# Score products of a chunked retention as 64 by 64 quarters instead of 64 by 128 halves

## The chip, the cores and the metric

The kernel runs on one core of one Trainium2 chip. The metric is the device time of one execution in microseconds (us), the median of several runs.

## What is computed

A retention layer (linear attention with a decay per head) and two MLPs behind it, all in fp32. The layer, with 2 sequences, 8 heads, 768 positions and 64 values per head:

```python
for t in range(S):
    state = gamma[None, :, None, None] * state + np.einsum('bhd,bhe->bhde', k[:, :, t], v[:, :, t])
    y[:, :, t] = scale * np.einsum('bhd,bhde->bhe', q[:, :, t], state)
```

Then x = y as 1536 tokens of 512 values, `h = x @ w_in; x = (h * tanh(softplus(h))) @ w_out`, and a second MLP with `h * cos(h)` in the middle, 2048 hidden values each.

## The kernel before

The retention is done in 12 chunks of 128 positions (6 for each sequence). For a chunk `g` TensorE does four sets of fp32 products, each for 4 pairs `a` of heads and both heads `e` of a pair:

- `att_scores` (line 319): scores transposed, keys by queries. A head has 64 of the 128 partitions of `qk` (its two heads lie one above the other). The stationary operand is k, 64 partitions by 128 keys, the moving operand q, 64 partitions by 128 queries. Each head of the pair writes a PSUM tile of its own, `ss[e]`.
- `att_inter` (line 365): what the carried state gives. Stationary is the state of a head, 64 by 64, moving its scaled q, 64 by 128. `rows(a, e)` puts the even pairs and the odd pairs crosswise, so that four products in a row stand in the four 64 by 64 quarters of the array.
- `att_update` (line 334): k and scaled v, 128 positions by 64 columns, added to the state's sum.
- `att_out` (line 375): v (128 by 64 columns) and the masked scores, 128 moving columns.

VectorE multiplies the scores with the decaying mask (`att_mask`, line 328, two for each chunk), ScalarE and GpSimd scale v (`att_vd`) and q (`att_qd`), ScalarE or VectorE read the state's sum (`att_state`), and both take the output into x (`att_x_high`, `att_x_low`). The chunk loads `qkv` (two halves of 512 KB each, `att_load`, line 281) go out on SyncE's queue in order, among them the first MLP weights.

The order of all work is made by a planner (`Plan`): each operation is entered with an engine, a guessed cost and what it needs; TensorE and, for the loads, SyncE keep the order in which operations are entered. Around the change that order is written out as a loop: scores one chunk ahead, then the chunk's other products.

```python
chunk_pre(0)
chunk_scores(0)
...
for n in range(NCHK):
    if n + 1 < NCHK:
        chunk_pre(n + 1)
        chunk_scores(n + 1)
    chunk_inter(n)
    chunk_update(n)
    chunk_out(n)
```

The first chunk of a sequence (0 and 6) has no `att_inter`, the last one (5 and 11) no `att_update`. Behind the last `att_out` the MLPs follow: `gemm1` (line 428 multiplies x and a slice of `w_in` into `ps_h`) and `gemm2` (line 451, `ps_o`), with fp32r operands in a high and a low part, 512 moving columns. The weights' parts are made on VectorE, ScalarE and GpSimd meanwhile (`w_high_part`, `w_low`, `w_low_part` at line 262).

## Time and profile before

| | |
|---|---|
| Median of 3 runs | 572.5 us (572.11 to 572.55) |
| The profiled execution | 573.28 us |
| Its span on the core | 571.5 us |
| TensorE matmuls (PE) busy | 565.8 us, 99% of the span, 3054 instructions |
| TensorE weight loads (PEld) busy | 468.4 us, 82% |
| VectorE (DVE) busy | 382.6 us, 67% |
| ScalarE (ACT) busy | 230.1 us, 40% |
| GpSimd (POOL) busy | 97.5 us, 17% |

The profile records one execution by the hardware. PE is a matmul, PEld the load of its stationary operand, which runs beside other matmuls; matmuls overlap, so a share of 99% says that there is hardly a gap, not that the array is at its peak. In a row of the trace `64*128` after the operation are the rows and columns of the array that it uses, `64x128 f32` the operand; "idle before" in square brackets is time in which the engine stood still just before, with what ended it. "SPq" is SyncE's queue of transfers.

### The profile page before, as it was taken

The numbers are of one execution on the slowest core, as the hardware profiler recorded it, in microseconds if no ns is written. First come the engines' busy times: TensorE is split into PE (matmuls) and PEld (weight loads), VectorE is DVE, ScalarE is ACT, GpSimd is POOL, SyncE is SP. The second block draws the span as 40 slices with busy tenths as digits, with TensorE's granted clock in tenths as the row PEclk, the third lists the DMA queues.
The fourth block names the chain that finished last, engine by engine and source line by source line (L and its number), as shares of the span: only waits on it lengthen the run. The fifth ranks groups of instructions, "written<-read, shape, count | busy, mean of one in ns | idle before, by whom it ended". The sixth has DMA issues, their size and how long they took to land.

```text
span 571.5 us, 7260 instructions
## 1 busy us (share of the span) xinstructions
PE 565.8 (99%) x3054; PEld 468.4 (82%) x3054; DVE 382.6 (67%) x416; ACT 230.1 (40%) x284; POOL 97.5 (17%) x74
## 2 busy tenths in 40 slices
PE   8999999999999999999999999999999999999997
PEld 6888888888888888888888888888888888888886
DVE  5779889662375427653487985898498894765462
ACT  3574543422303303214326465465345354354240
POOL 6680001111110301111101111032010312010000
PEclk9999999999999999999999999999999999999999
DMA  8982254422032200412021030304004010000113
GB/s 297 413 335 75 75 210 158 147 75 73 1 131 91 73 1 0 148 73 75 0 75 73 26 123 1 138 10 147 1 0 148 32 41 2 1 1 1 73 38 110
DMA packets 14721, 49.91 MB, mean 87 GB/s; under 512 B 1632, under 2 KB 2016, under 8 KB 14688
## 3 DMA queue, kind: packets, MB, share of 16 engines
q1 hardware_dynamic: 14688, 49.44, 23.4%
q8 instruction: 24, 0.39, 0.3%
q14 instruction: 9, 0.07, 0.0%
HBM read 46.29 MB, written 3.15 MB: 86 GB/s over the span
## 4 chain that ended last, share of the span: by engine, by line
PE 94%; DMA 4%; SPq 1%; ACT 0%; issue 0%; DVE 0%; ACTq 0%
PE ps_h L428 46%; PE ps_o L451 46%; DMA qkv<-qkv_dram 4%; SPq L294 1%; PE ps_y L381 1%; PE ps_y L370 1%; PE ps_s L325 1%; PE ps_u L341 0%; ACT vd L308 0%; ACT x L395 0%; DVE acc L517 0%; SPq L758 0%; ACT st L353 0%; ACTq L308 0%
## 5 line engine op out<-in xcount | busy, mean ns | idle before, releaser
L428 PE MATMUL ps_h<-x,wi 128*128 128x512 f32 x1152 | 264.8, 389 | 0.0
L428 PEld LDWEIGHTS ps_h<-x,wi 128*128 128x128 f32 x1152 | 216.1, 188 | 45.0 <-issue 0.2
L451 PE MATMUL ps_o<-wo,g 128*128 128x512 f32 (+1 forms) x588 | 132.5, 385 | 0.0
L451 PE MATMUL ps_o<-g,wo 128*128 128x512 f32 x576 | 132.3, 389 | 0.0
L451 PEld LDWEIGHTS ps_o<-wo,g 128*128 128x128 f32 x588 | 108.9, 188 | 22.1
L451 PEld LDWEIGHTS ps_o<-g,wo 128*128 128x128 f32 x576 | 108.1, 188 | 22.5
L494 DVE TENSOR_TENSOR g<-mish,g 128x1024 fp32r<-128x1024 f32 x24 | 33.4, 1393 | 59.2 <-ACT g L490 59.2
L262 POOL TENSOR_TENSOR wo<-mag,wo 128x1024 fp32r<-128x1024 f32 x14 | 35.8, 2557 | 212.8 <-ACT wo L248 212.8
L510 DVE TENSOR_TENSOR acc<-ps_o,acc 128x1024 f32<-128x1024 f32 x35 | 42.8, 1222 | 34.6 <-PE ps_o L451 34.4
L262 POOL TENSOR_TENSOR wi<-mag,wi 128x1024 fp32r<-128x1024 f32 x12 | 30.3, 2525 | 193.1 <-ACT wi L248 193.1
L461 ACT ACTIVATE mish<-ps_h 128x1024 f32<-128x1024 f32 (+1 forms) x25 | 24.9, 995 | 95.1 <-PE ps_h L428 95.1
L474 DVE SCALAR_TENSOR_TENSOR turns<-whole,turns 128x1024 f32<-128x1024 f32 x24 | 29.4, 1223 | 44.7 <-ACT whole L470 44.7
L466 ACT ACTIVATE turns<-ps_h,quarter 128x1024 f32<-128x1024 f32 x24 | 26.7, 1114 | 65.4 <-PE ps_h L428 65.1
L239 DVE SCALAR_TENSOR_TENSOR mag<-raw,mag 128x1024 uint32<-128x1024 uint32 (+1 forms) x38 | 42.2, 1110 | 1.1
L483 ACT ACTIVATE turns<-turns 128x1024 f32<-128x1024 f32 x24 | 25.5, 1062 | 34.8 <-DVE turns L480 34.6
L494 DVE TENSOR_TENSOR g<-turns,g 128x1024 fp32r<-128x1024 f32 x24 | 33.2, 1384 | 8.0 <-ACT g L490 8.0
L486 DVE TENSOR_TENSOR turns<-turns,ps_h 128x1024 f32<-128x1024 f32 x24 | 29.2, 1216 | 10.1 <-ACT turns L483 6.8
L254 DVE SCALAR_TENSOR_TENSOR mag<-raw,mag 128x1024 uint32<-128x1024 uint32 x26 | 33.7, 1301 | 0.4
L490 ACT CAST g<-turns 128x1024 fp32r<-128x1024 f32 x24 | 25.1, 1044 | 16.9 <-DVE turns L486 16.9
L248 ACT CAST wi<-mag 128x1024 fp32r<-128x1024 f32 (+1 forms) x20 | 17.5, 876 | 27.3 <-DVE mag L254 22.4
L470 ACT ACTIVATE whole<-turns,magic 128x1024 f32<-128x1024 f32 x24 | 27.7, 1153 | 0.8
L480 DVE TENSOR_SCALAR turns<-turns 128x1024 f32<-128x1024 f32 x24 | 27.0, 1126 | 0.8
(50 smaller groups left out, 330.2 us busy)
## 6 DMA issues: line engine op xcount, KB each, us to landing
qkv<-qkv_dram SPq DMA_DIRECT2D x24, 512.0 KB, 10.1
raw<-w1i_dram SPq DMA_DIRECT2D x16, 512.0 KB, 4.2
raw<-w1o_dram SPq DMA_DIRECT2D x16, 512.0 KB, 4.1
raw<-w2i_dram SPq DMA_DIRECT2D x16, 512.0 KB, 4.0
raw<-w2o_dram SPq DMA_DIRECT2D x16, 512.0 KB, 3.6
out_dram<-acc SPq DMA_DIRECT2D x11, 256.0 KB, 2.1
out_dram<-acc SPq DMA_DIRECT2D x2, 128.0 KB, 1.7
few<-consts_dram SPq DMA_DIRECT2D x1, 146.0 KB, 2.2
```

The source lines that it names most:

```text
L239: nc.vector.scalar_tensor_tensor(out=a, in0=high, scalar=0xC0000000, in1=a, op0=ALU.bitwise_and, op1=ALU.bitwise_or)
L254: nc.vector.scalar_tensor_tensor(out=w_all_of(it, single)[:, ns], in0=raw_t[it][:, ns, :, 0], scalar=29, in1=mag_t[it][:, ns], op0=ALU.log ...
L262: eng.tensor_sub(out=w[:, :, 1], in0=w_all_of(it, single)[:, ns].bitcast(F32), in1=w[:, :, 0].bitcast(F32))
L428: nc.tensor.matmul(h[:, 0 if h_tag(k) == "s" else f % 2, :], w[:, f % 2, a, kk * 128 : (kk + 1) * 128], x[:, b, kk, :], start=(a + b + kk ...
L451: nc.tensor.matmul(ps, lhs, rhs, start=(n == 0), stop=(n == 3 * GF - 1))
L466: nc.scalar.activation(out=t_t[k], in_=h_t[k], func=AF.Identity, scale=INV_2PI, bias=quarter)
L470: nc.scalar.activation(out=n_t[k], in_=t_t[k], func=AF.Identity, bias=magic)
L474: nc.vector.scalar_tensor_tensor(out=t, in0=n_t[k], scalar=MAGIC, in1=t, op0=ALU.subtract, op1=ALU.subtract)
L480: nc.vector.tensor_scalar(out=t, in0=t, scalar1=-0.5, scalar2=0.5, op0=ALU.max, op1=ALU.min)
L486: nc.vector.tensor_mul(out=t_t[k], in0=t_t[k], in1=h_t[k])
L494: nc.vector.tensor_sub(out=g[:, :, 1, :], in0=t_t[k], in1=g[:, :, 0, :].bitcast(F32))
L510: nc.vector.tensor_add(out=acc, in0=o_t[m * NG + G, j, p], in1=acc)
```

## The change

Each score product is cut in two along the keys: `t` takes 64 of the 128 keys as stationary columns, and writes the 64 partitions of the PSUM tile that belong to them. The moving operand is the same for both. So a chunk has 16 products of 64 by 64 with 128 moving columns instead of 8 of 64 by 128; in the four products that follow each other each stands in another quarter of the array. Nothing else is changed, and no cost or need that the planner sees.

```diff
         for a in range(NPAIR):
-            for e in range(2):
-                h = slice(D * e, D * e + D)
-                nc.tensor.matmul(ss[e][:, a, :], qk[h, a, 1, :], qk[h, a, 0, :], start=True, stop=True)
+            for t in range(2):
+                keys = slice(D * t, D * t + D)
+                for e in range(2):
+                    h = slice(D * e, D * e + D)
+                    nc.tensor.matmul(
+                        ss[e][keys, a, :], qk[h, a, 1, keys], qk[h, a, 0, :], start=True, stop=True, skip_group_check=True,
+                    )
```

On TensorE before, in the middle of the retention (`ps_s` are scores, `ps_y` an output with the carried state at line 370 and with masked scores at line 381, `ps_u` the state's sum; the sizes are those of the product's output):

```order
L381 MATMUL ps_y<-p,qkv 64x128 x8
L325 MATMUL ps_s<-qkv 128x128 x8
L341 MATMUL ps_u<-vd,qkv 64x64 x8
L381 MATMUL ps_y<-p,qkv 64x128 x8
L325 MATMUL ps_s<-qkv 128x128 x8
L370 MATMUL ps_y<-qd,st 64x128 x8
L341 MATMUL ps_u<-vd,qkv 64x64 x8
```

The same place with the change, whose lines are numbered a little higher:

```order
L385 MATMUL ps_y<-p,qkv 64x128 x8
L327 MATMUL ps_s<-qkv 64x128 x16
L345 MATMUL ps_u<-vd,qkv 64x64 x8
L385 MATMUL ps_y<-p,qkv 64x128 x8
L327 MATMUL ps_s<-qkv 64x128 x16
L374 MATMUL ps_y<-qd,st 64x128 x8
L345 MATMUL ps_u<-vd,qkv 64x64 x8
```

The sets of products stand in the same order; only the scores are 16 with an output of 64 by 128 instead of 8 with 128 by 128. The orders of the other engines are the same as before, instruction by instruction.

## Rows read from the trace of the kernel before

**Rows 1.** Page, slices: busy tenths in 40 slices of the span, granted clock, DMA engines.

```profile
PE   8999999999999999999999999999999999999997
...
PEclk9999999999999999999999999999999999999999
DMA  8982254422032200412021030304004010000113
```

**Rows 2.** Chain that ended last, in order of time: start us, us, what.

```profile
17.44 11.76 DMA qkv<-qkv_dram
...
29.28 0.61 ACT vd L308 x3
...
32.07 0.99 PE ps_y L370 x16
...
45.72 32.89 PE ps_h L428 x144
```

**Rows 3.** Waits of SyncE's queue, 0 to 60 us: total us, times, longest.

```profile
SPq L294 <- DMA qkv<-qkv_dram: 13.8, 13, 2.6
```

**Rows 4.** Timeline of weight loads, 31 to 46 us: start us, us, instructions [idle before].

```profile
34.48 0.97 PEld L325 LDWEIGHTS ps_s<-qkv 64*128 64x128 f32 x16 [0.17 <-issue]
35.58 0.43 PEld L370 LDWEIGHTS ps_y<-qd,st 64*64 64x64 f32 x16
36.17 0.55 PEld L341 LDWEIGHTS ps_u<-vd,qkv 128*64 128x64 f32 x16 [0.17 <-issue]
36.63 0.86 PEld L381 LDWEIGHTS ps_y<-p,qkv 128*64 128x64 f32 x16
37.66 0.97 PEld L325 LDWEIGHTS ps_s<-qkv 64*128 64x128 f32 x16 [0.17 <-issue]
...
40.84 0.97 PEld L325 LDWEIGHTS ps_s<-qkv 64*128 64x128 f32 x16 [0.17 <-issue]
...
44.02 0.43 PEld L370 LDWEIGHTS ps_y<-qd,st 64*64 64x64 f32 x16 [0.17 <-issue]
44.62 0.85 PEld L381 LDWEIGHTS ps_y<-p,qkv 128*64 128x64 f32 x16 [0.17 <-issue]
45.65 0.53 PEld L428 LDWEIGHTS ps_h<-x,wi 128*128 128x128 f32 x3 [0.17 <-issue]
```

**Rows 5.** Weight loads by line, 0 to 46 us: count | busy us, mean ns | idle.

```profile
L325 PEld LDWEIGHTS ps_s<-qkv 64*128 64x128 f32 x192 | 11.7, 187 | 3.8 <-DMA qkv<-qkv_dram 2.2 <-issue 1.4 <-PE ps_y L381 0.3
...
L370 PEld LDWEIGHTS ps_y<-qd,st 64*64 64x64 f32 x160 | 4.5, 132 | 1.7 <-issue 0.6
```

**Rows 6.** Timeline of weight loads, 9 to 32 us.

```profile
15.64 0.97 PEld L325 LDWEIGHTS ps_s<-qkv 64*128 64x128 f32 x16 [0.17 <-issue]
...
18.82 0.97 PEld L325 LDWEIGHTS ps_s<-qkv 64*128 64x128 f32 x16 [0.17 <-issue]
...
28.02 1.00 PEld L325 LDWEIGHTS ps_s<-qkv 64*128 64x128 f32 x16 [0.29 <-PE ps_y L381]
...
30.63 0.97 PEld L325 LDWEIGHTS ps_s<-qkv 64*128 64x128 f32 x16 [0.17 <-issue]
```

**Rows 7.** Timeline of ScalarE, 20 to 70 us.

```profile
35.35 2.04 ACT L308 ACTIVATE vd<-qkv,cst 128x64 f32<-128x64 f32 x8
37.27 0.93 ACT L353 ACTIVATE st<-ps_u,cst 128x64 f32<-128x64 f32 x4
```

**Rows 8.** Timeline of GpSimd, 20 to 70 us.

```profile
41.15 1.59 POOL L316 TENSOR_TENSOR qd<-qkv,cst 64x256 f32<-64x256 f32 x2
```

**Rows 9.** Timeline of VectorE, 20 to 70 us.

```profile
43.27 0.42 DVE L350 TENSOR_TENSOR st<-ps_u,cst 128x256 f32<-128x256 f32 x1 [0.40 <-PE ps_u L341]
43.62 0.68 DVE L332 TENSOR_TENSOR p<-ps_s,cst 128x512 f32<-128x512 f32 x1
...
45.15 0.69 DVE L262 TENSOR_TENSOR wi<-raw,wi 128x512 fp32r<-128x512 f32 x1
```

**Rows 10.** Windows, 46 to 60 us: busy us of PE, PEld, DVE, ACT, POOL, clock, DMA.

```profile
46.00:60.00 14.00, 14.00 (x63) 11.57 (x62) 13.59 (x24) 7.33 (x12) 0.00 (x0) 1.00 0.37 132
```

## The prediction

> **What bounds the kernel now.** I read the slices of the page first. TensorE is busy in nearly every slice and its granted clock is full in all of them, while the DMA engines are full in the first slices only [rows 1]. The changed line runs in the first 46 us, so the question is what bounds that stretch. The chain of waits answers in two parts [rows 2]. Up to 29.2 us the chain is loads of `qkv`; behind them stand 2.9 us on ScalarE (the scaled v of chunk 7, a copy of x, the state of chunk 6), and the first TensorE piece starts at 32.07 us. From there to the end the chain is TensorE without a gap. The loads keep their own pace: SyncE's queue waits on earlier loads 13 times, 13.8 us in all [rows 3]. So before 32.07 us time saved on TensorE is time it will wait; after it, time saved is time off the end.

> Which score products stand behind 32.07 us? In the list of weight loads by time, those of chunks 9, 10 and 11, which start at 34.48, 37.66 and 40.84 us, each followed by an `att_inter` [rows 4]. Those of chunks 0 to 8 stand ahead (chunk 8's at 30.63 us [rows 6]).

> How TensorE spends a chunk. Each fp32 product is executed as two passes: 12 chunks x 8 products = 96, and the row counts 192 [rows 5]. I read each phase from its first weight load to the next phase's first one, because that includes what lies between phases [rows 4]:
> - scores, 16 passes of 64 rows x 128 columns, two side by side: 34.48 to 35.58 = 1.10 us;
> - `att_inter`, 16 passes of 64x64, four side by side, 128 moving columns: 35.58 to 36.17 = 0.59 us, so four groups of four;
> - `att_update` and `att_out`, both 128 rows x 64 columns: 36.17 to 37.66 = 1.49 us;
> - `att_out` alone (the last, behind an `att_inter`): 44.62 to 45.65 = 1.03 us, eight groups of two with 128 moving columns.

> From the last two phases with 128 moving columns comes the price of a group, whatever stands in it: (1.03 - 0.59) / 4 = **0.11 us**, and 0.15 us that a phase costs besides (filling with its first 64-column weights, and emptying before the next shape). The rows also show that phases of one shape share this 0.15: `att_update` flows into `att_out` with no idle mark between their weight loads, while the loads behind a change of shape carry 0.17 us of idle time [rows 4]. (`att_inter` behind scores carries no mark because a score weight load is recorded with 187 ns, one of `att_inter` with 132 [rows 5], which covers it; the sum of the two phases is the better reading.)

> **The change, part by part.**

> *Products.* 96 become 192, so 384 passes and 384 weight loads instead of 192 each; per chunk 32 passes instead of 16. They go to four quarters of the array instead of two halves, so I count eight groups, as many as there are pairs now. The pair costs 0.11 us as well: eight pairs and 0.22 make 1.10. So the array gains nothing in throughput, as it was full before (64x128 twice); the moving columns are 128 either way. Price per group of four: no row shows these products so, but `att_inter` has the same tile, the same 128 moving columns and four side by side, so I take 0.11. The ends: below, the 0.06 us of a pair in `att_update`, which moves half the columns (1.49 less the 1.03 of `att_out`, over eight); above, 0.22, if quarters go two by two at today's price of a pair.

> *First weights.* The phase's fixed part goes from 1.10 - 8 x 0.11 = 0.22 to the 0.15 of a phase with 64-column weights: -0.07 us per chunk.

> *Change of shape.* Scores and the `att_inter` behind them now have one shape, so that the second fixed part goes: -0.15 us wherever `att_inter` follows. Scores and `att_inter` together are 36.17 - 34.48 = 1.69 us now; as one phase of twelve groups they take 1.03 + 4 x 0.11 = 1.47. **Gain 0.22 us per chunk** with an `att_inter` behind (chunks 2 to 6 and 8 to 11), 0.07 for the others (0, 1, 7). The change of shape from `att_out` to scores and that from `att_inter` to `att_update` both stay.

> *On the path:* chunks 9, 10 and 11, 3 x 0.22 = **0.66 us**. *Off it:* chunks 2 to 6 finish 5 x 0.22 = 1.1 us earlier and then wait for chunk 7's load; the score weights at 28.02 us already waited 0.29 [rows 6]. That wait grows to about 1.4 us and the gain is gone. Chunk 8's 0.22 ends in the wait for ScalarE's state that now ends at 32.07.

> *What is late next.* Nothing but TensorE's work changes its order, and no wait is added. Whatever feeds the last chunks must be ready 0.2 to 0.7 us sooner:
> - the state of chunk 8 on ScalarE ends at 37.27 + 0.93 = 38.20 and does not move, as ScalarE works without a break ahead of it; `att_inter` of chunk 9 would start its products at 37.44 + 0.05 + 8 x 0.11 = 38.37 [rows 4, 7]. 0.17 us to spare, the tightest place;
> - the scaled q of chunk 11 on GpSimd ends at 41.15 + 1.59 = 42.74, and is wanted at 44.02 - 0.66 = 43.36 [rows 4, 8];
> - VectorE's state of chunk 10 (43.27) waits for TensorE and so moves with it, and the masking of chunk 11 behind it, which ends at 44.30 for an `att_out` at 44.62, moves too [rows 4, 9];
> - the MLP starts at 45.65. Its first eight products need only what was ready before; the ninth, 8 x 0.228 = 1.8 us later (32.89 us over 144 [rows 2]), needs the low part that VectorE ends at 45.84 [rows 9]. 1.6 us to spare, and VectorE's work there is behind the masking that moves.
> From then on TensorE has no gap that could take the gain back, as its own pace sets everyone else's.

> *Sum:* -0.66 us. The profiled execution took 573.28 us (span 571.5), so it would take 572.62; that execution lies 0.78 above the median of the runs, 572.5, so against the median I predict **571.84 us**, a gain of 0.12%. Under 0.2% (1.15 us) a measurement of this kernel can't tell it from no change.

> **The rivals.**

> *A, slower: the quarters do not run four side by side.* Two of them share the same 64 partitions of q as moving data; if a pair of row groups is all that runs at once, every pass costs what it does now, 0.055 us, and scores take 16 groups. Scores and `att_inter` are then 20 groups, 1.03 + 12 x 0.11 = 2.35 instead of 1.69, +0.66 per chunk. Chunks 2 to 6 push the score weights of chunk 7 to 27.73 + 5 x 0.66 = 31.0 us. TensorE and not the loads sets the pace from then on: 1.91 for those scores, 1.49 for update and output, 2.35 for the next scores and `att_inter`, so that the `att_update` of chunk 7 starts at 36.8 us instead of 32.07 + 0.99 = 33.1 [rows 2]; the last three chunks add 2.0. +5.7 us, 578.2. It decides once a group of four costs over 0.137 us, where eight of them eat the 0.22. Against it: in `att_inter` two tiles on the same partitions run beside two others at 0.11 a group, and `att_update` issues 16 passes and 16 loads in 0.46 us (36.17 to 36.63 [rows 4]), 0.029 a pass where 0.137 would be 0.034. 0.06.
> [...]

> *B, the shared shape does not help:* a semaphore or the other tile order still empties the array between scores and `att_inter`. Then only the first weights gain, 3 x 0.07 = 0.21 us: 572.3. For it: no row shows these two phases joined. Against: the joined `att_update` and `att_out`, which also wait on semaphores in between. 0.08.

> *C, the gain is given back at the start of the MLP:* VectorE is busy 13.59 of the 14 us from 46 to 60 [rows 10]; if a weight's low part were late by as much as TensorE is early, the time stays 572.5. Against: the 1.6 us above. 0.07.

> *D, more gain:* if the stretch before 32 us were TensorE's after all, nine joins and three first weights count: 9 x 0.22 + 3 x 0.07 = 2.2 us, 570.3. For it: scores follow each other 3.18 us apart there too (15.64, 18.82 [rows 6]), TensorE's own pace. Against: the wait of 0.29 at 28.02 and the loads in the chain. 0.05.

> **How the numbers follow.** Forecast 0.72, A 0.06, B 0.08, C 0.07, D 0.05, 0.02 for anything else. The range takes in B and C above (572.5, and 0.2 for runs that scatter from 572.11 to 572.55) and below a gain of twice the forecast's: 571.2 to 572.7. The ends of the group's price lie outside it: 0.22 is A, and with 0.06 each of the three would gain 0.4 more, 570.6, which the equal moving columns speak against. Faster by over 0.2%: D and half of the forecast's edge by scatter, 0.09. Slower: A and a little scatter, 0.07. Within: 0.84.

> **What would show it.** In the changed profile: 384 score passes; score weights to the next `att_update` weights 1.47 us instead of 1.69 in chunks 9 to 11; `att_inter` without the 0.15 of its own; a wait of about 1.4 us ahead of the scores of chunk 7; the chain unchanged to 32.07 and `ps_h` starting near 45.06. Score phases near 1.9 us mean A, 1.62 for the two phases together B, a gap in `ps_h` after 45 us C, a first TensorE piece of the chain well before 32 us D.

## Result, and the profile after

The changed kernel is slower: 577.75 us median of 5 runs (576.66 to 578.14) against 572.27 for the kernel before, 5 runs as well, ratio 1.0092 with a 95% interval of 1.0081 to 1.0104. The forecast was 571.84 with a range up to 572.7; the time lies outside it, on the other side. Its profiled execution took 578.07 us, span 576.3 against 571.5.

The page, where it differs from [rows 1] and the table ahead: 384 instructions more on TensorE (192 matmuls, 192 weight loads), no more busy time, and two slices with less of it.

```profile
span 576.3 us, 7644 instructions
...
PE 564.8 (98%) x3246; PEld 468.1 (81%) x3246; DVE 382.8 (66%) x416; ACT 230.3 (40%) x284; POOL 97.4 (17%) x74
...
PE   8779999999999999999999999999999999999997
...
PEclk9999999999999999999999999999999999999999
...
q8 instruction: 25, 0.41, 0.3%
```

The chain of waits, in order of time, answers to [rows 2] (start us, us, what):

```profile
3.05 8.98 DMA qkv<-qkv_dram
...
12.08 1.10 PE ps_s L327 x32
...
19.75 0.43 PE ps_u L345 x9
20.19 1.72 issue
21.91 0.39 PE ps_u L345 x6
...
26.19 0.81 PE ps_s L327 x23
27.00 1.38 issue
28.38 0.54 PE ps_s L327 x9
...
32.90 0.80 PE ps_s L327 x20
33.71 1.71 issue
35.42 0.55 PE ps_s L327 x10
...
40.09 0.10 PE ps_y L385
40.19 1.69 issue
41.88 1.09 PE ps_y L385 x15
```

The loads and ScalarE are out of the chain after 12 us: it is TensorE from there on, and in it stand four gaps marked "issue", time in which the engine waited for nothing that the profile shows. They lie in the middle of a set of products, two in scores, one in an update, one in an output. With them the MLP starts at 50.45 us instead of 45.65 [rows 4], and +4.8 us is the whole difference of the spans.

The phases themselves are as forecast. The weight loads of the scores of chunk 10 (42.90) and what follows answer to [rows 4]:

```profile
42.90 0.86 PEld L327 LDWEIGHTS ps_s<-qkv 64*64 64x64 f32 x32 [0.17 <-issue]
43.72 0.48 PEld L374 LDWEIGHTS ps_y<-qd,st 64*64 64x64 f32 x16
44.37 0.55 PEld L345 LDWEIGHTS ps_u<-vd,qkv 128*64 128x64 f32 x16 [0.17 <-issue]
44.83 0.86 PEld L385 LDWEIGHTS ps_y<-p,qkv 128*64 128x64 f32 x16
...
50.45 1.69 PEld L432 LDWEIGHTS ps_h<-x,wi 128*128 128x128 f32 x8 [0.17 <-issue]
```

42.90 to 44.37 is 1.47 us for scores and `att_inter` together, 1.69 before. Four quarters run side by side and the shared shape saves its 0.15 us, as the sum had it.

### The profile page after: what moved, and what is told of

It is laid out like the page before. It is cut to its first block, busy times and chain, and to the rows that moved or that the text cites. A ratio compares the mean times of both kernels' runs of the same rounds, so it can differ in the third digit from the quotient of the medians.

```text
span 576.3 us, 7644 instructions
## 1 busy us (share of the span) xinstructions
PE 564.8 (98%) x3246; PEld 468.1 (81%) x3246; DVE 382.8 (66%) x416; ACT 230.3 (40%) x284; POOL 97.4 (17%) x74
## 4 chain that ended last, share of the span: by engine, by line
PE 96%; DMA 2%; issue 1%; SPq 0%; DVE 0%
PE ps_h L432 45%; PE ps_o L455 45%; PE ps_s L327 2%; PE ps_y L385 2%; DMA qkv<-qkv_dram 2%; PE ps_u L345 1%; PE ps_y L374 1%; SPq L294 0%; DVE acc L521 0%; SPq L762 0%
## 5 line engine op out<-in xcount | busy, mean ns | idle before, releaser
L490 DVE TENSOR_TENSOR turns<-turns,ps_h 128x1024 f32<-128x1024 f32 x24 | 29.2, 1216 | 10.1 <-ACT turns L487 6.8
L254 DVE SCALAR_TENSOR_TENSOR mag<-raw,mag 128x1024 uint32<-128x1024 uint32 x26 | 33.7, 1301 | 0.4
```

Of the source, the lines that this page charges most:

```text
L254: nc.vector.scalar_tensor_tensor(out=w_all_of(it, single)[:, ns], in0=raw_t[it][:, ns, :, 0], scalar=29, in1=mag_t[it][:, ns], op0=ALU.log ...
L490: nc.vector.tensor_mul(out=t_t[k], in0=t_t[k], in1=h_t[k])
```

## What the gaps have in common

Counted in the chain, from the end of the first gap to the next: 7 passes of the update, 16 of the output, 32 of scores, 16 and 16 and 16, 23 of scores. That is 126 passes, 252 matmuls and weight loads, and with four semaphore waits 256 instructions. The next two stretches are 256 as well: the gaps lie behind the recorded TensorE instructions 705, 961, 1217 and 1473. Queue 8 carries 25 transfers of 16 KB in this execution, 24 in the one before; 16 KB for 256 instructions are 64 bytes each. One of these transfers lies ahead of each gap's end; the transfer view of 19.4 to 20.4 us has

```profile
q8 instruction: 1, 0.02, 6.2%
```

The rivals: **I**, TensorE can't take in 164 instructions in 2.97 us, loads or no loads; **Q**, something in the quarters as such (their order, their PSUM tiles) holds it up.

## Experiments

**Without the later loads.** Two kernels, halves and quarters, with the same edit: chunks 5 to 11 are not loaded, their products read the data of chunks 2, 3 and 4.

```diff
     def att_load(g, lo, hi, eng=nc.sync):
+        if g > 4:
+            att[g] = att[2 + (g - 2) % 3]
+            return
```

> Scores as 64x128 halves, as before, but the loads of chunks 5 to 11 are left out (their products read chunks 2, 3 and 4 again). It is the base for the same edit with quarters. Theory F (TensorE's instructions arrive 256 at a time by a transfer of 16 KB that stands in line behind the loads): no gap of over 1 us on TensorE marked issue; the first MLP products start between 43.5 and 45.2 us instead of 45.65, since the wait for chunk 7's load is gone. Rival I (TensorE cannot take in its instructions faster, loads or no loads): the same for this form, as it has no gap before either.

> Scores as quarters, the loads of chunks 5 to 11 left out as in the base with halves. Theory F: the gaps of 1.4 to 1.7 us that the changed kernel shows at 27, 33.7 and 40.2 us vanish, as hardly a load is under way after 25 us; one near 20 us may stay, shorter. Scores and carried-state products together take 1.47 us per chunk, and the first MLP products start 1 to 2.2 us before those of the base with halves. Rival I: a gap of 1.4 to 1.7 us every 256 instructions all the same, the MLP 3 to 5 us later than in the base.

Measured: halves 572.06 us, MLP from 44.30; quarters 572.51, MLP from 44.82, one run each. With quarters one gap is left, 1.71 us at 22 us, while the loads still run; the three behind it are gone. The quarters' TensorE timeline, one chunk to the next, and the transfers from 26 to 44 us:

```profile
22.12 0.39 PE L348 MATMUL ps_u<-vd,qkv 128*64 128x64 f32 x6 [1.71 <-issue]
...
34.31 1.10 PE L330 MATMUL ps_s<-qkv 64*64 64x128 f32 x32
...
37.28 1.10 PE L330 MATMUL ps_s<-qkv 64*64 64x128 f32 x32
```

```profile
DMA packets 6, 0.08 MB, mean 5 GB/s; under 512 B 0, under 2 KB 0, under 8 KB 0
...
q8 instruction: 4, 0.07, 1.6%
```

A chunk takes 2.97 us, as with the loads, and nothing but instructions is transferred: the same instructions at the same rate run without a gap. That rules out I, and Q with it. My expectation for the MLP's start (1 to 2.2 us ahead of the halves) was missed, 0.5 behind: the gap that was left did not shorten. From the scores of chunk 6 on, ahead of which both have their waits, quarters need 44.82 - 26.33 = 18.5 us to the MLP, halves 44.30 - 24.66 = 19.6: 1.1 us gained in five chunks with a join and one without.

**More instructions, no quarters.** The scores stay halves; the output products are cut along the moving columns.

```diff
         for a in range(NPAIR):
-            for e in range(2):
-                nc.tensor.matmul(
-                    ps[rows(0, e), a % 2, a // 2, :], v[:, 2 * a + e, :], pm[g][:, e, a, :],
+            for cols in (slice(0, D), slice(D, C)):
+                for e in range(2):
+                    nc.tensor.matmul(
+                        ps[rows(0, e), a % 2, a // 2, cols], v[:, 2 * a + e, :], pm[g][:, e, a, cols],
```

> Scores as halves, as before; instead each output product is cut into two of 64 moving columns, in the array shape it had, so that a chunk has 160 matmul and weight-load instructions as with quarters, in about the array time of before (pairs of 64 columns cost 0.058 us, 16 x 0.058 = 0.93 instead of 8 x 0.11 = 0.88). Theory F: three to four gaps of 1 to 1.7 us marked issue, 256 instructions apart; the MLP starts 3 to 6 us later than before, 575 to 579 us. Rival Q (quarters as such hold TensorE up): no gap, 572.3 to 573.0.

Measured: 577.79 us, ratio 1.0094 (1.0079 to 1.0109), the same loss as with quarters. About 0.6 us of it is array time, as a chunk takes 3.24 us here instead of 3.18. The gaps in its TensorE timeline, their marks a little under the 1 to 1.7 us expected:

```profile
23.01 0.45 PE L382 MATMUL ps_y<-p,qkv 128*64 128x64 f32 x7 [0.97 <-issue]
29.73 1.03 PE L382 MATMUL ps_y<-p,qkv 128*64 128x64 f32 x26 [0.96 <-issue]
36.13 0.57 PE L341 MATMUL ps_u<-vd,qkv 128*64 128x64 f32 x13 [0.79 <-issue]
42.04 1.16 PE L325 MATMUL ps_s<-qkv 64*128 64x128 f32 x15 [0.86 <-issue]
```

They are at other places of the program and behind the same recorded instructions, 705, 961, 1217 and 1473. The count does it, not the shape.

**Still more instructions.** The carried-state products are cut in the same way too (192 instructions per chunk). Their start flags then come twice for a tile, and the output is no longer the layer's (relative error 0.22); the work and its waits are the same.

> Halves; output products and carried-state products both cut into two of 64 moving columns, so that a chunk has 192 instructions instead of 128 (160 with quarters). Theory F: 256 instructions take about 4.4 us instead of 4.75 with quarters, so the gaps behind recorded instructions 705, 961, 1217 and 1473 are longer than in the changed kernel by about 0.3 us each, with a fifth at 449 or 1729; MLP start 51 to 55 us, 579 to 583 us. Rival Q: no gap, at most 0.5 us slower than before.

Measured in one run: 581.3 us, MLP from 53.69, gaps at the same four instructions and no fifth. Time and start as expected. The idle marks are not longer than with quarters (1.28, 1.61, 1.24 and 1.42 us), as expected they would be; the blocks came a little faster on that chip, 5.9 to 6.4 us apart.

**Loads with less under way at a time.** First each load in two of 64 partitions, then, without that, in two of 512 columns, with quarters and with halves.

```diff
-        eng.dma_start(out=att[g][:, lo:hi], in_=qkv[g, :, lo:hi])
+        for p in (slice(0, 64), slice(64, 128)):
+            eng.dma_start(out=att[g][p, lo:hi], in_=qkv[g, p, lo:hi])
```

```diff
-    cuts = (0, 1024, 2048)
+    cuts = (0, 512, 1024, 1536, 2048)
```

> Quarters, and each load of 512 KB is cut in two of 64 partitions, so that about half the bytes are under way at a time (the queue holds eight loads). Theory F, if the 16 KB transfer waits behind what is under way: its wait falls by about 2 us, the gaps shrink from 1.4-1.7 to under 0.3 us, the MLP starts at 45 to 46.5 us, 571.5 to 573.5. If its wait does not depend on how much is queued: gaps and time as in the changed kernel, 577 to 578. Rival I: as the changed kernel too.

> Quarters; each chunk is loaded in four pieces of 512 columns instead of two of 1024, all 128 partitions, so that a row of a load is 2 KB instead of 4. Cutting the loads by partitions slowed the loads themselves to 250 GB/s and made things worse, so this cuts them the other way. Theory F, with the 16 KB transfer standing behind a number of load rows: its wait falls from 4 to 2-2.5 us, the gaps of TensorE vanish or fall under 0.5 us, the MLP starts at 45.0 to 46.0 us and the time is 571.5 to 573, if the loads keep 400 GB/s. If the wait goes by bytes or time: gaps and time as in the changed kernel, 577 to 578. If rows of 2 KB move slower: the wait for loads grows, 575 and more, with gaps marked DMA.

> Halves as before, loads in pieces of 512 columns: what the shorter rows do alone. If the loads keep their pace: as before, 572.0 to 572.8, no gap. If they are slower: 575 and more.

Measured: 596.07 us (ratio 1.043), 577.46 (1.0094) and 575.08 (1.0050). Loads of 64 partitions move 250 GB/s instead of 410. Two gaps of that kernel, and its stretch from 20 to 30 us (the last two numbers are the DMA share and GB/s):

```profile
28.73 0.51 PE L346 MATMUL ps_u<-vd,qkv 128*64 128x64 f32 x10 [2.97 <-issue]
38.13 0.55 PE L328 MATMUL ps_s<-qkv 64*64 64x128 f32 x11 [2.65 <-issue]
...
```

```profile
20.00:30.00 10.00, 6.46 (x157) 5.51 (x153) 4.19 (x7) 3.22 (x13) 6.67 (x9) 0.98 1.04 253
```

With slower loads a block takes longer, 7.9 to 9.4 us from one gap's end to the next, and the loads last until about 60 us, so that there are five gaps. Rows of 2 KB move at 363 GB/s between 20 and 40 us with halves, which by itself costs them 2.9 us and shows no gap marked issue (though the carried-state products at instruction 1473, which comes 1.40 us behind its transfer's end, take 1.15 us instead of 0.60); with quarters the gaps stay, the longest 1.71 us. There a load lands 5.8 us after its issue instead of 10.7, so about half the bytes were under way, in half the row, and the wait was no shorter. The loads of 64 partitions are no clean test of this, as they were slower themselves.

Where the wait lies can be read. In the changed kernel a transfer of instructions begins 3.9, 3.9, 4.5 and 3.9 us after the first instruction of the block ahead of it (that of the first gap's block at 19.40, behind 15.48); with quarters and the later loads left out, once the loads are through, 0.3 to 0.9 us. The transfer itself takes about 1 us in both. So under the loads it begins late; what it waits for, these runs don't show.

**Quarters where they were to pay, and where not.** The scores' cut depends on the chunk, `g > 8` or `g < 9`:

```diff
-            for t in range(2):
-                keys = slice(D * t, D * t + D)
+            for keys in [slice(0, D), slice(D, C)] if g > 8 else [slice(0, C)]:
```

> Quarters for chunks 9, 10 and 11 alone, halves for the others; loads as before. My blind sum without instruction supply: -0.66 us, the whole forecast gain, 571.7. Theory F: the third and fourth blocks of 256 are needed 0.6 to 1.5 us sooner than before, with the loads still running, so one or two gaps with 0.4 to 2.5 us in all: MLP start 45.1 to 47.5 us, 571.8 to 574.2.

> Quarters for chunks 0 to 8, halves for the last three. My blind sum: no change, as what is gained there waits for chunk 7's load. Theory F: the first three gaps as in the changed kernel (near 20, 27 and 34 us, 1.4 to 1.7 us each), the fourth gone or under 0.7; MLP start 48 to 49.8 us, 575 to 577.

Measured: 573.43 us, ratio 1.0022 (1.0013 to 1.0031), and 577.36 us, 1.0086 (1.0071 to 1.0101). Late quarters have one gap, and the MLP starts at 45.38 us, as theory F had it:

```profile
37.58 0.99 PE L326 MATMUL ps_s<-qkv 64*64 64x128 f32 x28 [0.68 <-issue]
```

It is behind instruction 1217. Over its chunk it costs 1.1 us, and chunk 11, with instruction 1473 in it, takes 0.3 us longer than 2.96 without a mark: more than the 0.66 us that the joins save. That is 0.7 us net; the rest of the 1.3 between the medians is open. Early quarters, for which the blind sum (the prediction's, without the supply of instructions) said no change, bring nearly the whole loss, a little more than theory F gave them (MLP from 50.42 us): gaps at 705, 1217 and 1473, the first of them 2.02 us. The gap expected at 961 is missing. The granted clock had fallen to 0.50 behind the first one (last section), so that the block lasted 6.3 us, and the next one's first instruction came 1.46 us behind its transfer's end, where the gaps end too.

**The last chunk alone,** and the kernel before on the same chip (`g == 11` in the edit above).

> Quarters for chunk 11 alone. Blind sum: -0.22 us. Theory F: 32 more instructions near the end of the loads; the block that was usable about 1 us before it was needed is needed 0.8 us sooner, so a gap of 0.2 us at most at instruction 1473: 571.9 to 572.4, no difference that can be measured. It is the version with the best chance to be no slower.

> The kernel before without an edit, for a trace from the same chip as the other two. No gap marked issue over 0.5 us; the MLP starts between 44.5 and 46 us.

Measured: 572.40 us, ratio 1.0003 (0.9993 to 1.0012), no gap marked issue; the kernel before there 571.76 in one run. The MLP starts at 44.22 and 44.11 us (44.5 to 46 had been expected of the kernel before). From its scores to the MLP chunk 11 takes 4.59 us with quarters and 4.80 with halves: the join's saving is there, and too small for the times to show. No version came out ahead of the kernel before.

## Why the prediction was wrong

- **The step that failed** is "*Products.* 96 become 192 ... So the array gains nothing in throughput": the 384 additional instructions were priced by the array alone, at nothing, and the price of bringing them in was left out. The nearest thing to it, "`att_update` issues 16 passes and 16 loads in 0.46 us", shows how fast instructions are dispatched that are already there; over 32 instructions it can't show a limit that binds over 256. The runs put in its place: a block of 256 takes 6.5 to 7 us to come while the loads run, and quarters use it up in 4.6.
- **"After it, time saved is time off the end"** and the sum of -0.66 us: the three joins of chunks 9 to 11 are there, 1.47 us each. The fourth gap lies among them, and the third just ahead.
- **"Chunks 2 to 6 finish 1.1 us earlier and then wait for chunk 7's load":** they finish later. Gaps one and two put TensorE behind the loads, so the load and ScalarE waits that were to hide everything ahead of 32 us are gone from the chain. That is why early quarters alone cost 5 us: 3.8 around their first gap, with the low clock behind it, and 1.4 and 0.8 at the other two. The mark of 0.29 us at 28.02, which the prediction read as a wait for the load, names TensorE's own output product, and 0.17 of it stands at any change of shape [rows 4, 6].
- **The balance:** the first instruction behind a gap starts 1.94, 1.65, 1.98 and 1.96 us after the last one ahead of it (the marks are shorter by the modelled end of a matmul). Over whole chunks, against the same chunks with quarters and without loads, the gaps cost 1.98, 1.69, 2.14 and 2.00 us, and chunk 3, at instruction 449, another 0.21 without a mark: 8.02 us. Against it stand 9 x 0.22 + 0.07 = 2.05 us of phases, 0.38 us by which chunk 2 began earlier, and 0.81 us that the kernel before waited from 28 to 33 us and the changed one does not. That leaves 4.78 us, where 4.8 were measured.
- **Rival A** gave 578.2 us, close to the 577.75 measured, for a reason that the trace refutes: the groups of four cost 0.11 us. What was right in it is that TensorE and no longer the loads would set the pace.
- **The margin could have been read.** In the kernel before queue 8 has a transfer from 35.93 to 36.94 us, and the first instruction of its block runs at 38.76. With the 1.5 us that every gap of the changed kernel shows between the two, 0.3 us were left; in the later run of the kernel before, on another chip, the tightest of these margins is nothing, a transfer's end at 22.03 and its first instruction at 23.54. The kernel before stood at the limit, without one idle mark for it. From the first instruction of a block to where the next could start, a transfer's end and 1.5 us, it took 4.4 to 6.1 us in the first trace and 4.6 to 7.1 in the second; so the 6.5 to 7 of the changed kernel are no constant of these loads.
- B, C and D are out: the shared shape helps, the MLP runs without a gap from its start, and nothing was gained ahead of 32 us.

## What to carry to other kernels

Count instructions as bytes that have to be fetched: in these traces 64 each, in blocks of 256. Where small products run beside saturated loads, compare how long 256 instructions of the engine last (here 6.2 us with halves, 4.6 with quarters) with how long a block takes then (6.5 to 7 us), and leave a margin: the tightest margin of the kernel before was 0.3 us in its first trace and nothing in its second, and no idle mark showed it. The gaps of 1.4 to 1.7 us marked "issue" in the middle of a set of products, 256 recorded instructions apart, were the sign of it here; splitting a product so that it fills the array as well as before lost 8.02 us in the gaps and saved 2.05 in its phases.

## What the runs showed of the hardware beside that

After the gap of 2.02 us in the kernel with early quarters the granted clock fell to 0.50 for the whole of 24 to 26 us; the four gaps of the changed kernel, 1.4 to 1.7 us, left it at 1.00. The windows of the kernel with early quarters (the number ahead of the DMA share is the clock):

```profile
22.00:24.00 2.00, 0.60 (x10) 0.60 (x12) 0.93 (x2) 0.57 (x3) 1.77 (x4) 0.82 1.04 414
24.00:26.00 2.00, 2.00 (x22) 1.67 (x24) 0.00 (x0) 1.10 (x5) 1.31 (x2) 0.50 1.03 410
...
28.00:30.00 2.00, 2.00 (x60) 1.83 (x60) 1.35 (x4) 1.62 (x6) 1.85 (x3) 1.00 1.02 404
```

In 24 to 26 us TensorE got through 22 matmuls, in 28 to 30 us, at a clock of 1.00, 60. The length of one gap does not settle it: with loads of 64 partitions the clock was 0.50 from 29.7 to 33.0 us, 46.8 to 50.0 and 57.0 to 60.3, behind gaps of 2.97, 1.55 (with two waits for loads just ahead) and 2.82 us, and 1.00 from 38.2 to 41.0 behind one of 2.65.

And phases of one array shape share what a phase costs besides its groups: scores and carried-state products together take 1.47 us instead of 1.69, while scores alone gain 0.07 (chunk 7 in the two kernels without the later loads, 1.03 us with quarters and 1.10 with halves).
